# Attention gradients for one query: the products with q and grad_out written as wide matmuls, their scores turned back by transposes

## The chip, the cores and the metric

The kernel runs on one core of one Trainium2 chip. The metric is the device time of one execution in microseconds; before the change the median of three runs is 1302.17 us (1299.8 to 1305.56). The engines of a core named here are TensorE (PE in the profile, with its weight loads as PEld), VectorE (DVE), ScalarE (ACT), GpSimd (POOL) and SyncE (SP). Each works through its own list of instructions in order; semaphores tie the lists together.

## The reference, cut to what matters

Attention with a single query per head, 2 x 32 heads, 8192 keys, head size 128, all in bfloat16, together with the gradients for q, k and v:

```python
B, H, Sq, Sk, D = 2, 32, 1, 8192, 128

def _fwd_reference(q, k, v):
    scale = q.shape[-1] ** -0.5
    scores = jnp.einsum("bhqd,bhkd->bhqk", q, k) * scale
    p = _softmax(scores, axis=-1)
    return jnp.einsum("bhqk,bhkd->bhqd", p, v)

def reference(q, k, v, grad_out):
    _out, _vjp = jax.vjp(_f, q, k, v)      # _f calls _fwd_reference
    _grads = _vjp(grad_out)
    return (_out, *_grads)                 # out, dq, dk, dv
```

For each head this is: scores s = K q, weights P = softmax(s * scale), out = P V, dP = V grad_out, dS = P (dP - sum(P dP)) * scale, dq = dS K, and the two large outputs dv = P grad_out (an outer product) and dk = dS q (another). K and V are 134 MB each and are read once; dk and dv are as large and are written once.

## The kernel before

The 64 heads are handled as 32 pairs. K (or V) of a pair is one tile of 128 partitions x 128 tokens x 128 numbers in the `ring`, 4096 KB; partitions 0 to 63 hold the first head of the pair, 64 to 127 the second. There are six ring tiles, so three pairs fit. The gradients take the place of the inputs: dV is written over V's tile and dK over K's; `outer` (L272) overwrites the chunks that the pair no longer needs, and `store` (L282) sends it out. `load` (L107) of pair g+3 goes into the tile that the store of pair g has emptied; loads are issued by SP, which waits in order for the landing of that store, and stores are issued by ACT between its other work.

The order is written out by hand (`manual_schedule`). An iteration h has 16 steps j, each with two half-steps u. Steps 0 to 7 go through K of pair h in chunks of 16 tokens per partition, steps 8 to 15 through V. Each half-step does, for 8 tokens per partition:

- `transposes` (L113): eight matmuls with the identity (L119) that turn 128 tokens x 128 numbers into 128 x 128 in PSUM, tile `tp` (two buffers);
- the eviction of `tp` to the bfloat16 tile `ev` (four buffers), by ACT (L126), or by DVE (L124) in the first half of steps 8, 9, 10 and 11;
- `products` (L129), one step later: eight times the turned block is loaded as the weights (L136) and two columns, q (or grad_out) of the pair's two heads, stream through. The results land in PSUM tile `sm` (scores) or `dp` directly with tokens on partitions, which is the layout that the later work wants.

While iteration h runs, the second half of pair h-1 is still under way: the counter s is j for the pair of this iteration and j + 16 for the pair before it. The softmax is spread over steps 8 to 11: `row_max` (L154), `all_max` (L159), `exps` (L165), `sums` (L185), `weights_v` (L205), which writes the weights `wz` and the doubled weights `P2` (`doubled`, L197). From s = 12 on, `weighted_rows` (L243) multiplies the weights with the rows of V (and later K) on PE: four matmuls of 512 columns with 16 weight columns each, placed in four column strips of the array, collected in PSUM tile `acc`. `outer` (L272) runs on DVE one step behind. `deltas` (L215) and `weights_k` (L229) do the same for dS when the products with grad_out are finished (steps 0 and 1 of the next iteration). `acc_to_sbuf` (L256) copies `acc` after step 6 of the next iteration, `combine` (L260) at step 8 folds it into the columns of out and dq, and `spread_row` (L140), with a copy by ACT (L152), spreads a row of q or grad_out over the partitions at steps 8 and 2. Which s does what is in these tables:

```python
    ACC_V = {12: (0, 1), 13: (2, 3), 14: (4, 5), 15: (6,), 16: (7,)}
    OUT_V = {12: (0,), 13: (1, 2), 14: (3,), 15: (4, 5), 16: (6,), 17: (7,)}
    ACC_K = {19: (0, 1), 20: (2, 3), 21: (4, 5), 22: (6, 7)}
    OUT_K = {19: (0, 1), 20: (2,), 21: (3, 4), 22: (5,), 23: (6, 7)}
    STORE = {18: 0, 24: 1}
```

The last pair stores its gradients in pieces of 1024 KB as they become ready; at the very end out and dq are turned and stored (L364 to L369).

Of the kernel before, what the change touches and what calls it, by code (L numbers as in the profile page):

```python
# [20 lines left out]
def kernel(  # L21
# [30 lines left out]
    masks.make_identity(nc, ident_f[:])  # L52
    ones_row = const.tile([1, P], F32)
    nc.vector.memset(ones_row[:], 1.0)
    block = const.tile([P, P], F32)
# [31 lines left out]
    acc = ps_one.tile([P, 4 * D], F32, name="acc", tag="acc")  # L87
    sm = ps_one.tile([P, 4 * P], F32, name="sm", tag="sm")
    dp = ps_one.tile([P, 4 * P], F32, name="dp", tag="dp")
    misc = ps_one.tile([P, 4 * P], F32, name="misc", tag="misc")  # L90
# [3 lines left out]
    nat = const.tile([BH, 2, D], BF16)  # L94
    wz = [const.tile([P, NT // 4, 16], BF16, name=f"wz{w}") for w in range(2)]

    class Pair:
# [11 lines left out]

    def scores(w):  # L110
        return (dp if w else sm)[:, 0 : 2 * NT].rearrange("p (s n) -> p s n", s=2)

    def transposes(g, j, u):  # L113
        x = pairs[g]
        w, c = divmod(j, NCH)
        tp = ps_tp.tile([P, HC, P], F32, name="tp", tag="tp")
        for i in range(HC):
            n = c * CH + u * HC + i
            nc.tensor.matmul(  # L119
                tp[:, i, :], lhsT=x.kv[w][:, n, :], rhs=ident_bf[:], start=True, stop=True  # L120
            )
        ev = evp.tile([P, HC, P], BF16, name="ev", tag="ev")
        if (j, u) in ((8, 0), (9, 0), (10, 0), (11, 0)):
            nc.vector.tensor_copy(out=ev[:], in_=tp[:])  # L124
        else:
            nc.scalar.copy(out=ev[:], in_=tp[:])  # L126
        x.ev[j, u] = ev

    def products(g, j, u):  # L129
        x = pairs[g]  # L130
        w, c = divmod(j, NCH)
        ev = x.ev.pop((j, u))
        cols = (qT_all, doT_all)[w][:, 2 * g : 2 * g + 2]
        for i in range(HC):
            n = c * CH + u * HC + i
            nc.tensor.matmul(  # L136
                scores(w)[:, :, n], lhsT=ev[:, i, :], rhs=cols, start=True, stop=True
            )

    def spread_row(g, w):  # L140
# [13 lines left out]
    def row_max(x):  # L154
        x.mp = work.tile([P, 1], F32, name="mp", tag="mp")
        for s, hs in enumerate(halves):
            nc.vector.reduce_max(out=x.mp[hs], in_=scores(0)[hs, s, :], axis=AX.X)  # L157

    def all_max(x):  # L159
        mT = sm[0:1, 2 * NT : 2 * NT + P]  # L160
        nc.tensor.transpose(mT, x.mp[:], ident_f[:])
# [3 lines left out]
    def exps(x):  # L165
        mb = sm[:, 2 * NT + P : 2 * NT + P + 2]
        nc.tensor.matmul(mb, lhsT=ones_row[:], rhs=x.gm[:], start=True, stop=True)  # L167
        negm = work.tile([P, 1], F32, name="negm", tag="negm")
        x.E = big.tile([P, NT], F32, name="E_f", tag="E_f")
        x.ld = work.tile([P, 2], F32, name="ld", tag="ld")  # L170
        for s, hs in enumerate(halves):
            nc.vector.tensor_scalar(
                out=negm[hs], in0=mb[hs, s : s + 1], scalar1=-scale, scalar2=None, op0=ALU.mult
            )
        for s, hs in enumerate(halves):
            nc.scalar.activation(  # L176
                out=x.E[hs],
                in_=scores(0)[hs, s, :],
                func=ACT.Exp,
                bias=negm[hs],  # L180
                scale=scale,
                accum_out=x.ld[hs, 0:1],
            )

    def sums(x, w):  # L185
        x.lsum = (dp if w else sm)[:, 2 * NT + P + 8 : 2 * NT + P + 9]
        nc.tensor.matmul(x.lsum, lhsT=block[:], rhs=x.ld[:, w : w + 1], start=True, stop=True)  # L187

    def to_weights(x, w, src, s1):
        for s, hs in enumerate(halves):  # L190
            nc.vector.tensor_scalar(  # L191
                out=wz[w][hs, :, 8 * w + 4 * s : 8 * w + 4 * s + 4],
                in0=src[hs].rearrange("p (m j) -> p m j", j=4),
                scalar1=s1[hs], scalar2=None, op0=ALU.mult,
            )

    def doubled(x, name, src, s1):  # L197
        t = big.tile([P, NT, 2], BF16, name=name, tag=name)
        nc.vector.tensor_scalar(
            out=t[:], in0=src[:].unsqueeze(2).to_broadcast([P, NT, 2]),  # L200
            scalar1=s1[:], scalar2=None, op0=ALU.mult,
        )
        return t
# [11 lines left out]
    def deltas(x):  # L215
        x.dSu = big.tile([P, NT], F32, name="dSu", tag="dSu")
        for s, hs in enumerate(halves):
            nc.vector.tensor_tensor_reduce(  # L218
                out=x.dSu[hs],
                in0=x.E[hs],  # L220
                in1=scores(1)[hs, s, :],
                scale=1.0,
# [6 lines left out]
    def weights_k(x):  # L229
# [5 lines left out]
        for s, hs in enumerate(halves):  # L235
            nc.vector.scalar_tensor_tensor(  # L236
                out=x.dSu[hs], in0=scores(1)[hs, s, :], scalar=negdelta[hs], in1=x.E[hs],
                op0=ALU.add, op1=ALU.mult,
# [55 lines left out]
    for t in wz:  # L294
        nc.gpsimd.memset(t[:], 0.0)
    nc.vector.memset(acc[:], 0.0)
    for src, dst in ((nat[:, 0, :], qT_all), (nat[:, 1, :], doT_all)):
        tps = ps_tp.tile([P, BH], BF16, name="tps", tag="tp")
# [3 lines left out]

    ACC_V = {12: (0, 1), 13: (2, 3), 14: (4, 5), 15: (6,), 16: (7,)}
    OUT_V = {12: (0,), 13: (1, 2), 14: (3,), 15: (4, 5), 16: (6,), 17: (7,)}
    ACC_K = {19: (0, 1), 20: (2, 3), 21: (4, 5), 22: (6, 7)}
    OUT_K = {19: (0, 1), 20: (2,), 21: (3, 4), 22: (5,), 23: (6, 7)}
    STORE = {18: 0, 24: 1}

    with tc.manual_schedule():
        for g in range(RING // 2):  # L310
            load(g, 0)
            load(g, 1)
        for h in range(NP + 1):
            y = pairs[h] if h < NP else None
            x = pairs[h - 1] if h else None
            for j in range(NS):
                at = [(z, zg, s) for z, zg, s in ((x, h - 1, j + NS), (y, h, j)) if z]
                for u in range(2):
# [6 lines left out]
                    if u == 0:  # L325
                        if y and j == 8:
                            spread_row(h, 0)
                        if x and j == 2:
                            spread_row(h - 1, 1)
                        if x and j == 8:  # L330
                            combine(h - 1)
                    else:
                        if y and j == 9:
                            all_max(y)
                        if y and j == 10:
                            exps(y)
                        if y and j == 11:
                            sums(y, 0)
                        if x and j == 1:
                            sums(x, 1)  # L340
                    if u == 1:
                        for z, zg, s in at:
                            for w, when in ((0, ACC_V), (1, ACC_K)):
                                for c in when.get(s, ()):
                                    weighted_rows(z, w, c)
                if y and j == 8:
                    row_max(y)
                if y and j == 11:
                    weights_v(y)
                if x and j == 0:  # L350
                    deltas(x)
                if x and j == 1:
                    weights_k(x)
                for z, zg, s in at:
# [4 lines left out]
                    for w, when in ((0, OUT_V), (1, OUT_K)):  # L359
                        for c in when.get(s, ()):  # L360
                            outer_and_store(zg, w, c)
                if x and j == 6:
                    acc_to_sbuf(x)
# [36 lines left out]
```

## Time and profile before

| what | before |
|---|---|
| median of three runs | 1302.17 us (1299.8 to 1305.56) |
| profiled execution: time, span | 1301.66 us, 1299.9 us |
| PE busy, weight loads | 1093.5 us, 936.6 us |
| DVE, ACT, POOL busy | 930.0 us, 906.3 us, 2.0 us |
| mean granted clock of TensorE | 0.850 |
| bytes moved by DMA | 539.64 MB, mean 415 GB/s |
| transposes L119 | 8192 matmuls, 721.9 us busy |
| products L136 | 8192 matmuls, 364.6 us busy; their weight loads 338.3 us |
| evictions | ACT 896 x 1020 ns, DVE 128 x 1225 ns |
| outer products on DVE L275 | 512 x about 1220 ns |
| copy of `acc` on DVE L258 | 32 x 692 ns |

The page has six parts: busy time by engine, the span in 40 slices, the DMA queues, the chain of work that ended last, the costliest groups of instructions with the idle time before them, and the DMA issues. From the trace come the same things for any stretch of time, and the instructions in order of time. A row of the order of time gives start, duration, engine, source line, operation, tiles and shapes, and in brackets the idle time ahead of it with what ended it. Matmul durations overlap, so the pace is read from start to start. The granted clock is 1.00 at full speed.

### The profile page before, as it was taken

The numbers are of one execution on the slowest core, as the hardware profiler recorded it, in microseconds if no ns is written. First come the engines' busy times: TensorE is split into PE (matmuls) and PEld (weight loads), VectorE is DVE, ScalarE is ACT, GpSimd is POOL, SyncE is SP. The second block draws the span as 40 slices with busy tenths as digits, with TensorE's granted clock in tenths as the row PEclk, the third lists the DMA queues.
The fourth block names the chain that finished last, engine by engine and source line by source line (L and its number), as shares of the span: only waits on it lengthen the run. The fifth ranks groups of instructions, "written<-read, shape, count | busy, mean of one in ns | idle before, by whom it ended". The sixth has DMA issues, their size and how long they took to land.

```text
span 1299.9 us, 42160 instructions
## 1 busy us (share of the span) xinstructions
PE 1093.5 (84%) x19044; PEld 936.6 (72%) x19044; DVE 930.0 (72%) x1355; ACT 906.3 (70%) x1091; POOL 2.0 (0%) x10
## 2 busy tenths in 40 slices
PE   4999899988888889888888887898888988889883
PEld 3777787776777778777677776677677877778771
DVE  0888788767867677767786676776677666776775
ACT  4887778767866678757686576876578666786761
POOL 0000000000000000000000000000000000000000
PEclk9999989889988788868898688988788777887876
DMA  9999999999999999999999999999999999999986
GB/s 404 417 425 424 429 427 432 427 430 430 429 429 427 427 426 420 427 430 403 426 429 427 429 400 429 432 423 423 414 393 420 416 405 410 410 421 419 404 348 268
DMA packets 19796, 539.64 MB, mean 415 GB/s; under 512 B 2464, under 2 KB 2464, under 8 KB 2464
## 3 DMA queue, kind: packets, MB, share of 16 engines
q10 hardware_dynamic: 10400, 268.51, 49.0%
q1 hardware_dynamic: 9216, 268.44, 48.8%
q8 instruction: 149, 2.44, 0.7%
q14 instruction: 31, 0.25, 0.0%
HBM read 268.47 MB, written 268.47 MB: 413 GB/s over the span
## 4 chain that ended last, share of the span: by engine, by line
DMA 63%; PE 24%; ACT 7%; DVE 3%; issue 2%; ACTq 0%; SPq 0%; DVEq 0%
DMA ring<-in_v_dram 43%; DMA out_dram<-ring 19%; PE tp L119 15%; ACT ev L126 5%; PE misc L264 3%; PE dp L136 2%; PE acc L247 1%; DVE ring L275 1%; DMA nat<-in_grad_out_dram 1%; PE sm L136 1%; DVE ev L124 1%; PE sm L167 1%; ACT E_f L176 1%; ACT row L152 1%; PE sm L187 0%
## 5 line engine op out<-in xcount | busy, mean ns | idle before, releaser
L126 ACT CAST ev<-tp 128x1024 bf16<-128x1024 f32 x896 | 865.4, 1020 | 287.0 <-PE tp L119 273.4
L119 PE MATMUL tp<-ident_bf,ring 128*128 128x128 bf16 x8192 | 721.9, 240 | 148.7 <-DMA ring<-in_v_dram 73.8
L119 PEld LDWEIGHTS <-ring 128*128 128x128 bf16 x8192 | 581.3, 108 | 286.7 <-issue 189.6
L136 PEld LDWEIGHTS <-ev 128*128 128x128 bf16 x8192 | 338.3, 100 | 7.3 <-issue 5.7
L275 DVE TENSOR_TENSOR ring<-row,dS 128x2048 bf16<-128x2048 bf16 x256 | 298.9, 1220 | 41.7 <-PE acc L247 39.9
L275 DVE TENSOR_TENSOR ring<-row,P 128x2048 bf16<-128x2048 bf16 x256 | 300.2, 1221 | 36.8 <-PE acc L247 35.8
L124 DVE CAST ev<-tp 128x1024 bf16<-128x1024 f32 x128 | 156.7, 1225 | 135.1 <-PE tp L119 131.6
L136 PE MATMUL dp<-doT_all,ev 128*128 128x2 bf16 x4096 | 185.7, 167 | 2.2 <-issue 1.4
L136 PE MATMUL sm<-qT_all,ev 128*128 128x2 bf16 x4096 | 178.9, 165 | 3.8 <-issue 3.7
L247 PE MATMUL acc<-ring,wz 128*16 128x512 bf16 x2048 | 167.8, 396 | 3.2 <-DVE wz L191 2.3
L152 ACT CAST row<-misc 128x128 bf16<-128x128 f32 x64 | 18.1, 282 | 81.5 <-PE misc L143 74.8
L264 PE MATMUL misc<-pick,accsb 128*128 128x4 f32 x256 | 52.0, 326 | 17.5 <-ACT row L152 11.2
L264 PEld LDWEIGHTS misc<-pick,accsb 128*128 128x128 f32 x256 | 49.2, 286 | 23.2 <-ACT row L152 16.0
L247 PEld LDWEIGHTS <-wz 128*16 128x16 bf16 x2048 | 31.2, 86 | 11.0 <-issue 2.7
L218 DVE CUSTOM_DVE_ANT_0 dSu<-E_f,dp 64x128 f32<-64x128 f32 x64 | 18.3, 285 | 28.5 <-PE dp L136 28.0
L157 DVE TENSOR_REDUCE mp<-sm 64x1 f32<-64x128 f32 x64 | 18.5, 289 | 21.9 <-PE sm L136 21.2
L268 DVE CAST colsT<-misc 128x4 bf16<-128x4 f32 x32 | 5.1, 161 | 31.8 <-PE misc L264 31.8
L176 ACT ACTIVATE E_f<-sm,negm 64x128 f32<-64x128 f32 x64 | 23.2, 363 | 1.7
L236 DVE SCALAR_TENSOR_TENSOR dSu<-dp,negdelta,E_f 64x128 f32<-64x128 f32 x64 | 22.4, 350 | 2.2
L258 DVE COPY accsb<-acc 128x512 f32<-128x512 f32 x32 | 22.1, 692 | 2.0 <-PE acc L247 1.0
L191 DVE TENSOR_SCALAR wz<-dSu,rl 64x128 bf16<-64x128 f32 x64 | 18.1, 283 | 2.1
L191 DVE TENSOR_SCALAR wz<-E_f,rl 64x128 bf16<-64x128 f32 x64 | 18.1, 283 | 1.7
(42 smaller groups left out, 197.6 us busy)
## 6 DMA issues: line engine op xcount, KB each, us to landing
out_dram<-ring ACTq DMA_DIRECT2D x62, 4096.0 KB, 45.9
ring<-in_k_dram SPq DMA_DIRECT2D x32, 4096.0 KB, 27.6
ring<-in_v_dram SPq DMA_DIRECT2D x32, 4096.0 KB, 27.8
out_dram<-ring ACTq DMA_DIRECT2D x8, 1024.0 KB, 11.3
out_dram<-rows ACTq DMA_DIRECT2D x2, 16.0 KB, 9.7
nat<-in_q_dram ACTq DMA_DIRECT2D x1, 16.0 KB, 11.0
nat<-in_grad_out_dram ACTq DMA_DIRECT2D x1, 16.0 KB, 15.4
```

What stands on the lines that cost most here:

```text
L119: nc.tensor.matmul(tp[:, i, :], lhsT=x.kv[w][:, n, :], rhs=ident_bf[:], start=True, stop=True)
L124: nc.vector.tensor_copy(out=ev[:], in_=tp[:])
L126: nc.scalar.copy(out=ev[:], in_=tp[:])
L136: nc.tensor.matmul(scores(w)[:, :, n], lhsT=ev[:, i, :], rhs=cols, start=True, stop=True)
L152: nc.scalar.copy(out=x.row[:], in_=pb)
L176: nc.scalar.activation(out=x.E[hs], in_=scores(0)[hs, s, :], func=ACT.Exp, bias=negm[hs], scale=scale, accum_out=x.ld[hs, 0:1],)
L191: nc.vector.tensor_scalar(out=wz[w][hs, :, 8 * w + 4 * s : 8 * w + 4 * s + 4], in0=src[hs].rearrange("p (m j) -> p m j", j=4), scalar1=s1[ ...
L236: nc.vector.scalar_tensor_tensor(out=x.dSu[hs], in0=scores(1)[hs, s, :], scalar=negdelta[hs], in1=x.E[hs], op0=ALU.add, op1=ALU.mult,)
L247: nc.tensor.matmul(acc[32 * g : 32 * g + 16, :], lhsT=wz[w][:, n // 4, :], rhs=rows[:, n : n + 4, :].rearrange("p n d -> p (n d)"), start= ...
L258: nc.vector.tensor_copy(out=x.accsb[:], in_=acc[:])
L264: nc.tensor.matmul(c, lhsT=x.accsb[:, j * D : (j + 1) * D], rhs=pick[:, j], start=(j == 0), stop=(j == 3),)
L275: nc.vector.tensor_tensor(out=x.kv[1 - w][:, n : n + CH, :].rearrange("p n (d t) -> p n d t", t=2), in0=row.unsqueeze(1).to_broadcast([P, ...
```

## The change

`products` no longer loads the turned block as weights. The two columns of q (or grad_out) become the weights, and the turned blocks stream: four blocks of 128 tokens, 512 columns, in one matmul. So that all chunks can share one PSUM tile, the two columns stand in a block of 16 that is otherwise zero; which two of the 16 depends on the chunk c, so that chunk c adds its scores into rows 2c and 2c+1 and zero into the others. The zero-padded weights are `qz` (one for q, one for grad_out, 8 x 18 columns), refilled for each pair by `stand` on GpSimd. A half-step issues two such matmuls, in column strips 2u and 2u+1 of the array, and the whole of K (or V) collects in one tile `raw`, started at c = 0 and stopped at c = 7.

The scores then lie with tokens along the free axis. `raw_to_sbuf` copies `raw` to SBUF on DVE (fp32, into a buffer of the `ev` pool), and `turn_scores` transposes it by four fp32 transposes into PSUM tile `turned`, one tile for both inputs. The order of the tokens in it is another, so everything that reads scores or writes weights has new access patterns, and `doubled` becomes two instructions. `row_max`, `all_max`, `exps`, `sums`, `weights_v`, `deltas`, `weights_k`, the tables and the stores move one step later; `acc_to_sbuf` moves from step 6 to 8 and `combine` from 8 to 9. VectorE evicts (3,0), (10,0), (11,0), (12,0) instead of (8,0), (9,0), (10,0), (11,0). The small PSUM results of the softmax move into `misc`. On DVE the order around step 8 is now: outers up to dK chunk 5, copy of `raw`, outers 6 and 7, copy of `acc`.

```diff
-    sm = ps_one.tile([P, 4 * P], F32, name="sm", tag="sm")
-    dp = ps_one.tile([P, 4 * P], F32, name="dp", tag="dp")
+    raw = ps_one.tile([P, 4 * P], F32, name="raw", tag="raw")
+    turned = ps_one.tile([P, 4 * P], F32, name="turned", tag="turned")
...
+    qz = [const.tile([P, 8 * 18], BF16, name=f"qz{w}") for w in range(2)]
...
-    def scores(w):
-        return (dp if w else sm)[:, 0 : 2 * NT].rearrange("p (s n) -> p s n", s=2)
+    def scores(s):
+        hs = halves[s]
+        return turned[hs].rearrange("p (k r z) -> p z k r", k=16, z=2)[:, s, :, 0:8]
+
+    def by_rounds(t):
+        return t.rearrange("p (k r) -> p k r", r=8)
+
+    def by_tokens(t):
+        return t.rearrange("p (i g r) -> p r g i", i=4, g=4)
...
-        if (j, u) in ((8, 0), (9, 0), (10, 0), (11, 0)):
+        if (j, u) in ((3, 0), (10, 0), (11, 0), (12, 0)):
             nc.vector.tensor_copy(out=ev[:], in_=tp[:])
...
+    def stand(g, w):
+        cols = (qT_all, doT_all)[w][:, 2 * g : 2 * g + 2]
+        nc.gpsimd.tensor_copy(
+            out=qz[w][:].rearrange("p (r c) -> p r c", c=18)[:, :, 0:2],
+            in_=cols.unsqueeze(1).to_broadcast([P, 8, 2]),
+        )
...
-        for i in range(HC):
-            n = c * CH + u * HC + i
-            nc.tensor.matmul(
-                scores(w)[:, :, n], lhsT=ev[:, i, :], rhs=cols, start=True, stop=True
-            )
+        for i in range(2):
+            k = 2 * u + i
+            nc.tensor.matmul(
+                raw[32 * k : 32 * k + 16, :],
+                lhsT=qz[w][:, 16 * c : 16 * c + 16],
+                rhs=ev[:, 4 * i : 4 * i + 4, :].rearrange("p n d -> p (n d)"),
+                start=(c == 0),
+                stop=(c == NCH - 1),
+                tile_position=(0, 32 * k),
+            )
+
+    def raw_to_sbuf(x):
+        x.raw = evp.tile([P, 4 * P], F32, name="rawsb", tag="ev")
+        nc.vector.tensor_copy(out=x.raw[:], in_=raw[:])
+
+    def turn_scores(x):
+        for i in range(4):
+            own = slice(i * P, (i + 1) * P)
+            nc.tensor.transpose(turned[:, own], x.raw[:, own], ident_f[:])
...
     def doubled(x, name, src, s1):
         t = big.tile([P, NT, 2], BF16, name=name, tag=name)
-        nc.vector.tensor_scalar(
-            out=t[:], in0=src[:].unsqueeze(2).to_broadcast([P, NT, 2]),
-            scalar1=s1[:], scalar2=None, op0=ALU.mult,
-        )
+        for k in range(2):
+            nc.vector.tensor_scalar(
+                out=t[:, :, k].rearrange("p (r g i) -> p r g i", g=4, i=4),
+                in0=by_tokens(src[:]), scalar1=s1[:], scalar2=None, op0=ALU.mult,
+            )
         return t
...
-    ACC_V = {12: (0, 1), 13: (2, 3), 14: (4, 5), 15: (6,), 16: (7,)}
-    OUT_V = {12: (0,), 13: (1, 2), 14: (3,), 15: (4, 5), 16: (6,), 17: (7,)}
-    ACC_K = {19: (0, 1), 20: (2, 3), 21: (4, 5), 22: (6, 7)}
-    OUT_K = {19: (0, 1), 20: (2,), 21: (3, 4), 22: (5,), 23: (6, 7)}
-    STORE = {18: 0, 24: 1}
+    ACC_V = {13: (0, 1), 14: (2, 3), 15: (4, 5), 16: (6,), 17: (7,)}
+    OUT_V = {13: (0,), 14: (1, 2), 15: (3,), 16: (4, 5), 17: (6,), 18: (7,)}
+    ACC_K = {20: (0, 1), 21: (2, 3), 22: (4, 5), 23: (6, 7)}
+    OUT_K = {20: (0, 1), 21: (2,), 22: (3, 4), 23: (5,), 24: (6, 7)}
+    STORE = {19: 0, 25: 1}
+    stand(0, 0)
...
-                        if x and j == 2:
+                        if x and j == 3:
                             spread_row(h - 1, 1)
-                        if x and j == 8:
+                        if x and j == 9:
                             combine(h - 1)
                     else:
                         if y and j == 9:
+                            turn_scores(y)
+                        if y and j == 10:
                             all_max(y)
-                        if y and j == 10:
+                        if y and j == 11:
                             exps(y)
-                        if y and j == 11:
+                        if y and j == 12:
                             sums(y, 0)
                         if x and j == 1:
+                            turn_scores(x)
+                        if x and j == 2:
                             sums(x, 1)
...
+                if y and j == 4:
+                    stand(h, 1)
+                if h + 1 < NP and j == 12:
+                    stand(h + 1, 0)
                 if y and j == 8:
+                    raw_to_sbuf(y)
+                if x and j == 0:
+                    raw_to_sbuf(x)
+                if y and j == 9:
                     row_max(y)
-                if y and j == 11:
+                if y and j == 12:
                     weights_v(y)
-                if x and j == 0:
+                if x and j == 1:
                     deltas(x)
-                if x and j == 1:
+                if x and j == 2:
                     weights_k(x)
...
-                if x and j == 6:
+                if x and j == 8:
                     acc_to_sbuf(x)
```

## The prediction

> **What bounds the kernel now.** I read the page's part 1 and 2 first, then the DMA queues, then the chain, then the busy time by stretches, and last the order of time inside two early pairs. The page:
>
> ```profile
> span 1299.9 us, 42160 instructions
> DMA  9999999999999999999999999999999999999986
> q10 hardware_dynamic: 10400, 268.51, 49.0%
> q1 hardware_dynamic: 9216, 268.44, 48.8%
> q8 instruction: 149, 2.44, 0.7%
> DMA 63%; PE 24%; ACT 7%; DVE 3%; issue 2%; ACTq 0%; SPq 0%; DVEq 0%
> ```
>
> Loads and stores together fill the 16 DMA engines for 97.8% of the span, so a pair (four transfers of 4096 KB, 16.78 MB) costs 39.0 us at the 430 GB/s of the best slices and 40.4 us at the mean of 415. The engines' shares (PE 84%, ACT 70%) look far away. The stretches show how far:
>
> ```profile
> 80.00:120.00 40.00, 36.63 (x702) 30.88 (x699) 33.47 (x51) 33.34 (x41) 0.00 (x0) 0.96 1.00 417
> 1000.00:1040.00 40.00, 34.72 (x574) 29.86 (x571) 27.91 (x42) 27.27 (x34) 0.00 (x0) 0.79 1.00 410
> ```
>
> (columns: PE, weight loads, VectorE, ScalarE, GpSimd busy; then granted clock, DMA share, GB/s). Early, with three pairs loaded ahead, 702 matmuls fit in 40 us at clock 0.96; later 574 at 0.79. Two successive `combine` groups (L264) start at 65.70 and 100.13: compute alone needs 34.4 us per pair. Between the first V transposes of pair 1 (64.38) and of pair 31 (1251.39) lie 30 pairs of 39.6 us. So DMA sets the pace, and compute has 39.6 - 34.4 = 5.2 us to spare per pair. The question is whether the change uses up more than that. The order of time in an early pair:
>
> ```profile
> 111.12 6.90 DVE L275 TENSOR_TENSOR ring<-row,P 128x2048 bf16<-128x2048 bf16 x6 [0.55 <-PE acc L247]
> 111.88 0.61 PE L119 MATMUL tp<-ident_bf,ring 128*128 128x128 bf16 x8
> 112.32 0.34 PE L136 MATMUL dp<-doT_all,ev 128*128 128x2 bf16 x8
> 112.60 0.61 PE L247 MATMUL acc<-ring,wz 128*16 128x512 bf16 x8
> 113.14 0.62 PE L119 MATMUL tp<-ident_bf,ring 128*128 128x128 bf16 x8
> 116.54 0.39 PE L247 MATMUL acc<-ring,wz 128*16 128x512 bf16 x4
> 116.86 0.10 PEld L119 LDWEIGHTS <-ring 128*128 128x128 bf16 x1 [0.23 <-issue]
> ...
> 63.23 0.69 DVE L258 COPY accsb<-acc 128x512 f32<-128x512 f32 x1
> 63.84 2.35 DVE L275 TENSOR_TENSOR ring<-row,dS 128x2048 bf16<-128x2048 bf16 x2
> 64.38 0.61 PE L119 MATMUL tp<-ident_bf,ring 128*128 128x128 bf16 x8 [0.33 <-ACT ev L126]
> 65.70 1.06 PE L264 MATMUL misc<-pick,accsb 128*128 128x4 f32 x8 [0.36 <-ACT row L152]
> 66.61 0.61 PE L119 MATMUL tp<-ident_bf,ring 128*128 128x128 bf16 x8
> 68.38 0.61 PE L119 MATMUL tp<-ident_bf,ring 128*128 128x128 bf16 x8 [0.98 <-ACT ev L126]
> 69.03 1.01 PE L119 MATMUL tp<-ident_bf,ring 128*128 128x128 bf16 x8
> ```
>
> From start to start at full clock: eight transposes 0.44 us, eight products 0.20, a `weighted_rows` group of four 0.27 (0.32 alone; the next weight load waits for it). ScalarE's evictions follow each other every 0.98 us and pace most half-steps. The 1.01 us row is the half clock (0.86 from start to start), which holds from 69.0 to 72.8 after PE had paused only 0.36 and 0.98 us.
>
> **The change part by part.** I write (j,u) for half-step u of step j, T for its eight transposes, P for its products. Sums are per pair against the 34.4 us.
>
> Products. Per half-step 8 weight loads and 8 two-column matmuls go; 2 loads of 16 columns and 2 matmuls of 512 columns in two column strips come. Nearest row: a lone L247 group, 0.32 us; with two strips I take 0.30 against 0.20. Bounds: 0.21 (the streaming alone) to 0.52 (the two one after the other). Under ScalarE's 0.98 pace it is hidden (0.44 + 0.30). It shows in the seven steps with two L247 groups, 2 x 0.74 + 0.54 = 2.02 against ScalarE's 1.96: from T(4,1) to T(8,0) I get 7.2 us against 6.65 (before, a late pair: 1038.95 to 1045.6, where V then makes PE wait): **+0.55**.
>
> V section, first half. The order on VectorE is now: copy of `raw`, the last two dK outers (6 and 7), copy of `acc`; before, `acc` was copied two steps ahead of `combine`. `combine` at (9,0) stands on PE behind T(8,0), P(7,0), T(8,1), P(7,1), T(9,0), P(8,0). From T(8,0): P(7,1) ends at 1.65; semaphore 0.15, `raw` 0.69, outers 2.35, `acc` 0.69, 0.1: `combine` at 5.6, done at 6.4, then T(9,1). Before it was 64.38 to 69.03 = 4.65: **+1.75**. PE and then ScalarE sit idle some 2.7 us. P(8,0) itself waits for the `raw` copy (one PSUM tile serves both inputs), inside this time.
>
> V section, second half. The turn adds four fp32 transposes after P(8,1). Their cost has no row: per transpose, bounded below by an fp32 weight load of 0.10 (L264: eight passes in 0.80) and above by a half-clock load and stream in series, 0.19 + 0.23 = 0.42. I take 0.16 at full clock, nearer the L264 pace since loads can overlap, so 0.65 per turn. Then (10,0), (11,0), (12,0) go to VectorE at 1.23 each with the maximum, exponent and sum steps one step later. Walking the waits, T(12,0) starts 11.6 us after T(8,0) with no slow clock; before 74.75 - 64.38 = 10.4, of which the 3.8 us at half clock cost about 1.7. After an idle stretch of 2.7 us I expect half clock again, over `combine` (+0.7), T(9,1) and its products (+0.6), the turn and one more half-step (+0.7): 2.0 us, so 13.6. First and second half together: **+3.2** (without slow clock +1.2).
>
> K section. VectorE now runs, from the last dO product on: `raw` copy 0.12 + 0.69, two outers 2.35, `deltas` 0.65, an outer 1.2, negdelta and `dSu` 1.0, `wz` 0.6, the two halves of `doubled` 0.6 (a 128-element row is 0.28, before one of 0.35), an outer 1.2, and only then the eviction of (3,0), 8.4 to 9.65. T(3,0) is done about 5.5, and P(3,0) stops PE until 9.7. T(0,0) to T(4,1) becomes 11.7 us against 9.67 (47.73 to 57.40), the second turn included: **+2.1**. PE is half idle for 4 us there, so half clock may follow in the PE-paced steps: 0 to 1.5, I take **+0.75**.
>
> Last quarter, T(12,0) to the next T(0,0): 7.8 against 8.0: **0** (one more eviction on VectorE, products slower).
>
> Sum 34.4 + 0.55 + 3.2 + 2.1 + 0.75 = **41.0 us per pair**. Low end, clock never slow: 38.1. High end: slow clock for 8 us after each V, as in the last pair of before (1252.7 to 1260.6), and products 0.1 dearer where PE paces: 44.
>
> Costed at nothing: `stand`, 64 small GpSimd copies four steps or more ahead of their use (cover: those steps; price without it about 0.2 each, as GpSimd's 128x128 memset). The stores, their issues on ACT's queue and the loads behind them on SP move a step and the stall later, about 4 to 6 us; the cover is the store queue, 45.9 us to landing where 4096 KB alone at 415 GB/s take 10.1. Without it the DMA would run dry for those 4 to 6 us, twice a pair. The products go from 16,384 instructions to 4096, some 900 others come: 27% of 42,160 fewer, which shorten q8's 0.7% (9 us) by 2.5 us, worth something only if DMA still bounds.
>
> Ends. Pair 0 takes 30.8 us (16.9 to 47.7), now about 2.5 more: T(8,0) of pair 1 at 69 instead of 64.4. From T(8,0) of pair 31 to the end were 48.5 us; the V section, a `raw` copy and turn ahead of `deltas` (+2) and `acc` copied after the last outers make it 53.
>
> **Sum.** 69 + 30 x 41.0 + 53 = 1352 us of span. Around the span lie 1.8 us (profiled run 1301.66, span 1299.9), and that run is 0.5 below the median 1302.17: **1354 us**.
>
> **Rivals.** *DMA still covers it.* If compute stays under 39.6 us per pair, last V lands where it did, less 2.5 for instruction traffic, plus 4.5 of tail: 1302 + 2 = 1304. For it: a 100% DMA share and a walk whose margin over 39.6 is only 1.4 us. Against: two stalls that follow from in-order queues. Chance 0.10.
>
> *The clock stays full.* If PE never falls to half clock, the sum is 38.1, again under DMA's 39.6, and the time about 1304. Against it is the fall at 69.0 after pauses of 0.36 and 0.98 us, which the coming stall of 2.7 exceeds. Chance 0.05. The Trainium skill, "TensorE: Matmul & The Clock Gate", section "HAM oscillation — how this bites in real kernels", asks for no PE gaps above about 3.4 us; by that rule the 2.7 us stall would be harmless and this rival right, but the trace disagrees, with half clock after 0.98.
>
> *Faster.* The other side: the products now stream 512 columns, so PE is denser at half clock and returns sooner; V waits (73.8 us in 25 pairs) and the half-clock spells of some 13 us per late pair shrink, stores issue earlier and DMA holds its best rate. It decides once compute stays under 38 us per pair, and gives 64 + 30 x 39.0 + 53 + 2 = 1289. Against: DMA was full at 410 GB/s too. Chance 0.07.
>
> *Worse.* Products one after the other, or long half clock: above 42.6 us per pair, beyond 1400, with 44 us 1444. Chance 0.12.
>
> **How the numbers follow.** Forecast 0.66, between 39.6 and 42.6 us per pair. Range 1300 to 1400: it takes in the hidden cases and leaves out 0.07 below and 0.12 above. No change means within 0.5%, 6.5 us, about what can be measured here: 0.10, the hidden cases' larger part. Slower 0.66 + 0.12 + 0.05 = 0.83, faster 0.07.
>
> **What the profile after would show.** DMA share near 0.95 with V waits almost gone; `combine` starts about 41 us apart; `combine` waiting for the VectorE copy of `acc` some 2.5 us in each pair; PE waiting at the products for the VectorE eviction of (3,0); clock about 0.8 to 0.9 in all stretches. I am wrong if V waits stay at 2 us per pair (DMA still bounds) or if product pairs take 0.45 us or more.

## The result, and the profile after

| | before | after |
|---|---|---|
| median | 1303.87 us (1299.8 to 1307.04, 4 runs) | 1431.26 us (1430.55 to 1433.02, 4 runs) |
| profiled execution: time, span | 1301.66 us, 1299.9 us | 1430.55 us, 1428.8 us |
| granted clock, mean | 0.850 | 0.902 |
| mean GB/s | 415 | 377 |
| time per pair, first to 31st start of `combine` | 39.6 us | 43.7 us |

The ratio is 1.0981, 95% interval 1.0946 to 1.1016. The kernel became slower, as forecast, by 127 us where 52 were forecast; 1431 lies above the range of 1300 to 1400.

The page of after, its first line, the DMA row of the 40 slices, the queues and the stores:

```profile
span 1428.8 us, 30765 instructions
...
DMA  9989999989999999999999998999989999999947
...
q1 hardware_dynamic: 9216, 268.44, 47.5%
q10 hardware_dynamic: 10400, 268.51, 44.6%
q8 instruction: 103, 1.69, 0.4%
...
out_dram<-ring ACTq DMA_DIRECT2D x62, 4096.0 KB, 19.9
```

Loads and stores together have fallen from 97.8% of the span to 92.1%, and a store now lands 19.9 us after its issue instead of 45.9. With two stores in each pair, 45.9 us were more than two stores under way at once, 19.9 us in pairs of 43.7 are about one. DMA follows; compute leads. The same two stretches as before (PE, weight loads, VectorE, ScalarE, GpSimd busy; granted clock, DMA share, GB/s):

```profile
80.00:120.00 40.00, 34.69 (x389) 20.39 (x388) 30.01 (x42) 27.91 (x33) 0.40 (x2) 0.93 0.91 368
1000.00:1040.00 40.00, 34.66 (x380) 20.89 (x378) 28.67 (x41) 27.04 (x34) 0.40 (x2) 0.91 0.93 384
```

Early and late are alike, which they were not before: there is no stock of loaded pairs that runs out. The waits (total, times, longest):

```profile
ACT ev L134 <- PE tp L127: 400.0, 433, 14.9
...
PE misc L296 <- DVE accsb L290: 88.7, 32, 8.9
...
DVE rawsb L161 <- ACT row L180: 57.5, 31, 1.9
PE raw L150 <- DVE ev L132: 47.0, 31, 1.5
```

PE's waits for V and K, 73.8 and 5.2 us before, are gone from the list. In their place stand two waits for VectorE, one of each kind per pair: `combine` for the copy of `acc`, and `products` for the eviction of (3,0). The first one in the order of time:

```profile
594.19 0.62 PE L127 MATMUL tp<-ident_bf,ring 128*128 128x128 bf16 x8
...
595.78 0.39 PE L150 MATMUL raw<-ev,qz 128*16 128x512 bf16 x2
...
596.10 0.62 PE L127 MATMUL tp<-ident_bf,ring 128*128 128x128 bf16 x8
596.27 0.69 DVE L161 COPY rawsb<-raw 128x512 f32<-128x512 f32 x1 [1.89 <-ACT row L180]
...
596.88 2.35 DVE L307 TENSOR_TENSOR ring<-row,dS 128x2048 bf16<-128x2048 bf16 x2
...
597.01 0.39 PE L150 MATMUL raw<-ev,qz 128*16 128x512 bf16 x2 [0.29 <-DVE rawsb L161]
...
599.14 0.68 DVE L290 COPY accsb<-acc 128x512 f32<-128x512 f32 x1
...
599.97 1.84 PE L296 MATMUL misc<-pick,accsb 128*128 128x4 f32 x8 [2.58 <-DVE accsb L290]
...
601.67 1.01 PE L127 MATMUL tp<-ident_bf,ring 128*128 128x128 bf16 x8
...
602.62 0.60 PE L150 MATMUL raw<-ev,qz 128*16 128x512 bf16 x2
...
603.15 1.12 PE L166 MATMUL turned<-ident_f,rawsb 128*128 128x128 f32 x4
```

Read down the VectorE rows: copy of `raw`, two outers, copy of `acc`, and only then `combine`, 2.58 us after PE had nothing else to do. The last four rows are PE at half clock (`combine` 1.84 us instead of 1.06, transposes 1.01 instead of 0.62). The second wait, with the store's issue that the ScalarE queue holds in front of an eviction:

```profile
626.79 0.61 PE L127 MATMUL tp<-ident_bf,ring 128*128 128x128 bf16 x8 [0.84 <-ACT ev L134]
...
627.65 1.23 DVE L132 CAST ev<-tp 128x1024 bf16<-128x1024 f32 x1
...
628.08 1.01 ACT L134 CAST ev<-tp 128x1024 bf16<-128x1024 f32 x1 [1.34 <-DVE ring L307]
...
628.92 0.39 PE L150 MATMUL raw<-ev,qz 128*16 128x512 bf16 x2 [1.52 <-DVE ev L132]
...
629.80 1.26 PE L279 MATMUL acc<-ring,wz 128*16 128x512 bf16 x8
...
630.99 1.03 PE L127 MATMUL tp<-ident_bf,ring 128*128 128x128 bf16 x8
```

Again a stall, and behind it half clock. And a step of after where PE is never short of work, with the weight loads:

```profile
612.91 0.62 PE L127 MATMUL tp<-ident_bf,ring 128*128 128x128 bf16 x8
613.46 0.39 PE L150 MATMUL raw<-ev,qz 128*16 128x512 bf16 x2
613.78 0.62 PE L127 MATMUL tp<-ident_bf,ring 128*128 128x128 bf16 x8
614.33 0.39 PE L150 MATMUL raw<-ev,qz 128*16 128x512 bf16 x2
614.34 0.81 PE L279 MATMUL acc<-ring,wz 128*16 128x512 bf16 x8
615.08 0.62 PE L127 MATMUL tp<-ident_bf,ring 128*128 128x128 bf16 x8
```

From start to start: transposes to products 0.55 us, products to transposes 0.32, products with a group of eight `weighted_rows` 0.75; the whole step 2.17 us.

### The profile page after: what moved, and what is told of

It reads as the page before. It is cut to its first block, busy times and chain, and to the rows that moved or that the text cites. A ratio compares the mean times of both kernels' runs of the same rounds, so it can differ in the third digit from the quotient of the medians.

```text
span 1428.8 us, 30765 instructions
## 1 busy us (share of the span) xinstructions
PE 1228.6 (86%) x13220; PEld 751.7 (53%) x13220; DVE 986.0 (69%) x1451; ACT 925.4 (65%) x1091; POOL 15.1 (1%) x76
## 5 line engine op out<-in xcount | busy, mean ns | idle before, releaser
L127 PE MATMUL tp<-ident_bf,ring 128*128 128x128 bf16 x8192 | 683.3, 231 | 26.6 <-ACT ev L134 26.2
L127 PEld LDWEIGHTS <-ring 128*128 128x128 bf16 x8192 | 523.7, 104 | 280.3 <-issue 273.1
L150 PE MATMUL raw<-ev,qz 128*16 128x512 bf16 x2048 | 414.8, 401 | 59.3 <-DVE ev L132 47.0
L279 PE MATMUL acc<-ring,wz 128*16 128x512 bf16 x2048 | 225.9, 404 | 1.2 <-DVE wz L219 1.2
L150 PEld LDWEIGHTS <-qz 128*16 128x16 bf16 x2048 | 98.8, 86 | 174.3 <-issue 76.7
L161 DVE COPY rawsb<-raw 128x512 f32<-128x512 f32 x64 | 44.3, 692 | 121.4 <-PE raw L150 63.8
L296 PE MATMUL misc<-pick,accsb 128*128 128x4 f32 x256 | 50.8, 322 | 88.7 <-DVE accsb L290 88.7
L279 PEld LDWEIGHTS <-wz 128*16 128x16 bf16 x2048 | 51.1, 88 | 34.8 <-issue 9.4
L166 PE MATMUL turned<-ident_f,rawsb 128*128 128x128 f32 x256 | 55.7, 355 | 0.6 <-DVE rawsb L161 0.6
L166 PEld LDWEIGHTS turned<-ident_f,rawsb 128*128 128x128 f32 x256 | 35.4, 175 | 21.3 <-issue 20.2
L215 PE MATMUL misc<-ld,block 128*128 128x1 f32 x128 | 24.5, 260 | 1.8 <-DVE ld L249 1.8
L204 ACT ACTIVATE E_f<-turned,negm 64x128 f32<-64x128 f32 x64 | 23.2, 362 | 1.6
## 6 DMA issues: line engine op xcount, KB each, us to landing
out_dram<-ring ACTq DMA_DIRECT2D x62, 4096.0 KB, 19.9
```

Of the source, the lines that this page charges most:

```text
L127: nc.tensor.matmul(tp[:, i, :], lhsT=x.kv[w][:, n, :], rhs=ident_bf[:], start=True, stop=True)
L150: nc.tensor.matmul(raw[32 * k : 32 * k + 16, :], lhsT=qz[w][:, 16 * c : 16 * c + 16], rhs=ev[:, 4 * i : 4 * i + 4, :].rearrange("p n d -> ...
L161: nc.vector.tensor_copy(out=x.raw[:], in_=raw[:])
L166: nc.tensor.transpose(turned[:, own], x.raw[:, own], ident_f[:])
L204: nc.scalar.activation(out=by_rounds(x.E[hs]), in_=scores(s), func=ACT.Exp, bias=negm[hs], scale=scale, accum_out=x.ld[hs, 0:1],)
L279: nc.tensor.matmul(acc[32 * g : 32 * g + 16, :], lhsT=wz[w][:, n // 4, :], rhs=rows[:, n : n + 4, :].rearrange("p n d -> p (n d)"), start= ...
```

## The experiments

The theory to test: the loss is two waits that the in-order queues make, and the half clock behind each. The rivals: the wide products are themselves dear; the later stores starve DMA; the moved order alone is the loss. The measure that tells most is the time per pair, from one start of `combine` to the next; where neither transfers nor the clock interfere, it mostly repeats to 0.02 us.

**The copy of `acc` a step earlier.**

```diff
-                if x and j == 8:
+                if x and j == 7:
                     acc_to_sbuf(x)
```

> The changed kernel with one edit: the copy of acc is issued after step 7 instead of after step 8, so that on VectorE it stands ahead of the copy of raw and of outers 6 and 7. Theory (stalls): combine waits 2.6 us per pair for that copy and the half clock behind it costs another 2 to 3 us (combine 1.84 instead of 0.8, then the next transposes, products and the turn); both go, 43.7 us per pair becomes about 39, and the time falls from 1431 to between 1303 (DMA's floor) and 1350. Rival (products): TensorE's 0.87 us per half-step, with a switch to column strips and back, sets the pace and the gap is only moved: not below 1400.

Measured: 1298.41 us (10 runs), ratio to before 0.9987 (0.9968 to 1.0005). One moved line takes away 133 us and puts the time a little below the 1303 to 1350 expected. `combine` waits once, 6.6 us at the start of the run, and not again; the wait for (3,0) stays at 47.0 us. The first five pairs take 37.76 us each, later ones up to 42 us, in which PE waits for K again (18.8 us in 13 waits) or runs at half clock behind the smaller stall; stores land after 37.9 us.

**(3,0) evicted by ScalarE.**

```diff
-        if (j, u) in ((3, 0), (10, 0), (11, 0), (12, 0)):
+        if (j, u) in ((10, 0), (11, 0), (12, 0)):
```

> The changed kernel with one edit: the block of (3,0) is evicted by ScalarE instead of VectorE, so ScalarE has one more eviction (0.98 us) and the products of (3,0) no longer wait behind VectorE's long row of work. Theory (stalls): 1.5 us of wait and about 1.3 us of half clock in steps 4 to 7 go, 3 us per pair, time about 1340 (1320 to 1370). Rival (products): the wait moves to the next eviction, not below 1400.

Measured: 1348.91 us (4 runs), ratio 1.0363 (1.0348 to 1.0379), pairs of 40.23 to 41.59 us; `combine` still waits 88.7 us. So the smaller stall is worth 82 us by itself, with the half clock that follows it.

**Both.**

> Both edits, the early copy of acc and ScalarE evicting (3,0). Theory (stalls): 43.7 less 5 less 3 is under DMA's 39.6 us per pair, so the time meets DMA's floor, 1300 to 1312, the same as the kernel before. Rival (products): TensorE alone keeps it above 1380. Rival (later stores): the stores are still issued one step later than before, and if that is what costs, the time stays above 1400.

Measured: 1293.06 us (4 runs), ratio 0.9940 (0.9922 to 0.9957): with the two waits gone, the changed kernel is 0.6% faster than before, and below the 1300 to 1312 expected. The first seven pairs take 36.4 to 36.6 us each, later ones about 40. PE waits for K and V again (total, times, longest):

```profile
PE tp L127 <- DMA ring<-in_k_dram: 45.4, 22, 3.0
PE tp L127 <- DMA ring<-in_v_dram: 16.2, 13, 1.5
```

DMA sets the pace here. Neither the products nor the stores' steps were touched, which ends the later stores as the cause of the 127 us, and dear products as the whole cause. It does not show that the products are cheap: what they cost lies under the cover of DMA here.

**PE kept at work in the larger stall.** Six repeats of T(9,1), into the tile that the real ones then overwrite with the same values, stand ahead of `combine`. The stall stays; PE isn't idle in it.

```diff
+                            if y:
+                                keep_busy(h, 9, 1, 6)
                             combine(h - 1)
...
```

> The changed kernel with the wait of combine left as it is, but TensorE kept busy in it: the eight transposes of (9,1) are issued six times more, into the same PSUM buffer, ahead of combine (6 x 0.44 = 2.6 us). It separates the stall from the slow clock. Theory (stalls and slow clock): the stall stays, the half clock behind it goes, 2 to 3 us per pair less, 1340 to 1375. If the slow clock is of no account: 1425 to 1440. If the repeated work delays combine: above 1440.

Measured: 1365.29 us (4 runs), ratio 1.0497 (1.0479 to 1.0514), 66 us less than after although PE does 48 matmuls more in each pair. The pairs come in three sizes, near 40.39, 41.65 (to 41.86) and 43.07 us. The clock records of the trace tell them apart: a pair of the first size has no half clock in it, one of the second has a spell of 3.41 us (182.91 to 186.32, for one), one of the third a spell of 6.83 us (346.75 to 353.57).

**Only the products.** The kernel before with the two wide strips, written to `sm` and `dp`.

```diff
-        for i in range(HC):
-            n = c * CH + u * HC + i
+        for i in range(2):
+            k = 2 * u + i
             nc.tensor.matmul(
-                scores(w)[:, :, n], lhsT=ev[:, i, :], rhs=cols, start=True, stop=True
+                (dp if w else sm)[32 * k : 32 * k + 16, :],
+                lhsT=qz[w][:, 16 * c : 16 * c + 16],
+                rhs=ev[:, 4 * i : 4 * i + 4, :].rearrange("p n d -> p (n d)"),
...
```

> The kernel before, with its order of steps, its evictions on VectorE and its copy of acc untouched; only the products are the two strips with 512 streamed columns, written into sm and dp. The scores are then not turned: what the later steps read from sm and dp is not the scores, so the turning (raw copy, four transposes) is left out of the time. Theory (in-order stalls and the half clock behind them): wide products alone add some 0.2 us in each half-step that PE paces and no stall, so compute stays at 35 to 36.5 us per pair, under the transfers' 39.6, and the time is 1290 to 1306, against 1302 before. Rival (the wide products are themselves slow, one after the other or dearer to switch to): at least 42 us per pair and above 1370.

Measured: 1286.83 us (4 runs), ratio 0.9877 (0.9849 to 0.9905), a little below what was expected and the shortest time of all; the copies of `raw` and the turn are left out of it. The first five pairs take 34.8 to 34.9 us where before took 34.4 to 35.7. The granted clock from 40 to 240 us is 1.00, before it was 0.95. So in place, wide products cost next to nothing net: they are longer, but PE keeps its clock. The sections of the first five pairs show both sides. From T(12,0) to T(0,0), T(0,0) to T(4,1) and T(4,1) to T(8,0), where both kernels run at clock 1.00, the means go from 8.05, 9.35 and 7.03 us to 8.47, 9.70 and 7.40, 1.1 us more in all. From T(8,0) to T(12,0), where before runs at a mean clock of 0.70 to 0.84 and this kernel at 1.00, the mean goes from 10.64 to 9.25, 1.4 us less.

**Only the moved order.** The old products with the later tables, the later softmax steps, `acc` copied at step 8, `combine` at step 9, and VectorE's evictions as in after.

```diff
-        if (j, u) in ((8, 0), (9, 0), (10, 0), (11, 0)):
+        if (j, u) in ((3, 0), (10, 0), (11, 0), (12, 0)):
...
-                        if x and j == 8:
+                        if x and j == 9:
                             combine(h - 1)
...
-                if x and j == 6:
+                if x and j == 8:
                     acc_to_sbuf(x)
...
```

> The kernel before with its old products, and with all that the change moves: the later tables for outers and stores, acc copied at step 8 and combine at step 9, the steps on scores one later, VectorE's evictions at (3,0), (10,0), (11,0), (12,0). No raw copy and no turn. It computes the same. Theory: combine now waits for VectorE (outers 2.35, acc copy 0.69) but without the raw copy's 0.69 and its wait ahead, so about 1.0 to 1.8 us instead of 2.58; the wait for (3,0) shrinks in the same way to under 1 us. Compute 36.5 to 39.5 us per pair, still hidden: 1295 to 1320. It needs both the moved order and the added VectorE work to reach 43.7 us. Rival (the moved order is the whole loss): 42 us or more per pair, above 1370.

Measured: 1304.92 us (10 runs), ratio 1.0029 (1.0015 to 1.0044). The waits are there, but short; one row of its order of time:

```profile
146.62 1.03 PE L264 MATMUL misc<-pick,accsb 128*128 128x4 f32 x8 [0.94 <-DVE accsb L258]
```

0.94 us instead of 2.58. The first seven pairs take 35.4 to 37.9 us, mean 36.6, and DMA covers them. The moved order alone is not the loss; it needs what else the change adds, the copies of `raw`, the turns and the longer half-steps.

**Four strips together.** After, with the products of both half-steps behind the second one's transposes.

```diff
-                    if y and j:
-                        products(h, j - 1, u)
-                    elif x and j == 0:
-                        products(h - 1, NS - 1, u)
+                    for v in range(2 * u):
+                        if y and j:
+                            products(h, j - 1, v)
+                        elif x and j == 0:
+                            products(h - 1, NS - 1, v)
```

> The kernel after, with the four strips of a step issued together behind the second half-step's transposes, instead of two behind each: one change from full-width weights to 16-column strips per step instead of two. Theory: the two stalls stay, and each step that PE paces gets 0.2 to 0.35 us shorter (one exposed weight load of 0.11 and part of a 0.32 group saved), some 7 to 16 steps: 1 to 3 us per pair, 1340 to 1400, if the products' later place makes no new wait; the evicted blocks are held half a step longer, which may give part back. Rival (the change of strips costs nothing; only stalls and clock do): 1420 to 1440.

Measured: 1346.94 us (4 runs), ratio 1.0347 (1.0322 to 1.0373), 84 us less than after, with both stalls still in place and `combine`'s longer (106.1 us in 32). Pairs average 41.0 us, at 39.3, 40.8 or 42.8. At full clock in both kernels, the section from T(12,0) to T(0,0), which has no stall, takes 7.67 us instead of 8.46 in after, and T(4,1) to T(8,0) 7.06 instead of 7.81. So part of the loss does come from the products, as the rival of dear products had it, through the changes between the whole array and the strips. Two successive waits for (3,0) in its order of time show what differs:

```profile
595.42 0.61 PE L127 MATMUL tp<-ident_bf,ring 128*128 128x128 bf16 x8 [1.90 <-DVE ev L132]
595.95 0.39 PE L150 MATMUL raw<-ev,qz 128*16 128x512 bf16 x4
...
596.71 1.70 PE L127 MATMUL tp<-ident_bf,ring 128*128 128x128 bf16 x16
...
636.09 0.61 PE L127 MATMUL tp<-ident_bf,ring 128*128 128x128 bf16 x8 [1.90 <-DVE ev L132]
636.62 0.39 PE L150 MATMUL raw<-ev,qz 128*16 128x512 bf16 x4
...
637.38 1.07 PE L127 MATMUL tp<-ident_bf,ring 128*128 128x128 bf16 x16
```

The same wait of 1.90 us, once with half clock behind it (16 transposes in 1.70 us), once without (1.07).

**All three.** The copy of `acc` earlier, (3,0) on ScalarE, four strips together.

> The kernel after with acc copied a step earlier, (3,0) evicted by ScalarE, and the four strips of a step together. Theory: transfers bound it already without the fours (1293.06), so 1288 to 1298, combine starts 39.5 to 40.3 us apart once the loads ahead are used up, below 36.4 us early in the run. Rival (the compute side still sets the time): below 1280.

Measured: 1289.82 us (4 runs), ratio 0.9904 (0.988 to 0.9928). The first four pairs take 34.18 us, less than before's shortest, then DMA leads at about 40. Against the 36.43 us of the first pairs with both stalls removed, all at clock 1.00, putting four strips together is worth 2.25 us per pair. Of the versions that do the whole computation this has the shortest time, 1.0% below before.

**PE kept at work in both stalls, first try.** Three repeats of T(4,1) ahead of P(3,0), beside the six of T(9,1).

```diff
+                    if y and x and j == 4 and u == 0:
+                        keep_busy(h, 4, 1, 3)
                     if y and j:
                         products(h, j - 1, u)
```

> The kernel after with both stalls left in and PE kept at work in them: the six repeats of T(9,1) ahead of combine, and three repeats of T(4,1) ahead of P(3,0). Theory: the half clock has two homes, behind combine and behind the wait for (3,0). With only the first filled, pairs took 40.39 us where no half clock followed (3,0) and 41.65 to 43.07 where it did. Filled in both places every pair should take 40.4 us: 1338 to 1350, granted clock 0.98 or more. What is then left above the 36.43 us of the kernel without either stall, 4.0 us, is the stalls themselves. Rival (the longer pairs come from something other than the clock): 1355 to 1370, pairs of 41.65 and 43.07 still there.

Measured: 1396.97 us (4 runs), ratio 1.0730 (1.0703 to 1.0756), outside both expectations. The repeats didn't fall into the stall; this row of its order of time shows why:

```profile
614.45 1.95 PE L147 MATMUL tp<-ident_bf,ring 128*128 128x128 bf16 x24 [1.51 <-DVE ev L135]
```

Their PSUM tile comes free with the same eviction of (3,0) that PE was waiting for. The stall of 1.51 us stayed empty and 1.4 us of work came behind it: pairs of 41.82 (40.39 + 1.43) and of 43.3 us. It says nothing on the clock.

**PE kept at work in both stalls, second try.** The repeats are of T(4,0), just ahead of the wait and with its tile free.

```diff
-        for i in range(HC):
-            n = c * CH + u * HC + i
+        for i in range(4 * HC if g and (j, u) == (4, 0) else HC):
+            n = c * CH + u * HC + i % HC
...
```

> As the last one, with the second filling where it can run: the transposes T(4,0), which stand just ahead of the wait for (3,0) and whose tile is free, are issued four times over (the tile is rewritten with the same values), 3 x 0.44 = 1.3 us of work inside a wait of 1.51. The six repeats of T(9,1) ahead of combine stay. Theory: no half clock behind either stall, so all pairs take the 40.4 us that the undisturbed pairs of the kernel with one filling took: 1338 to 1352, granted clock 0.98 or more. Rival (pairs of 41.65 and 43.07 have another cause): they stay, 1355 to 1370.

Measured: 1330.80 us (4 runs), ratio 1.0223 (1.0197 to 1.0249); mean clock 0.992. That is below the 1338 to 1352 expected, though the pairs are the 40.4 us that were expected. The sizes of 41.65 and 43.07 us are gone: nearly every pair takes 40.38 to 40.40 us. Rows of its order of time, and one stretch:

```profile
597.40 2.85 PE L147 MATMUL tp<-ident_bf,ring 128*128 128x128 bf16 x48
600.09 1.01 PE L311 MATMUL misc<-pick,accsb 128*128 128x4 f32 x8
...
624.40 1.95 PE L130 MATMUL tp<-ident_bf,ring 128*128 128x128 bf16 x32 [0.84 <-ACT ev L137]
```

```profile
240.00:1200.00 960.00, 924.34 (x11523) 597.46 (x11522) 730.02 (x1073) 686.83 (x811) 9.45 (x47) 1.00 1.00 416
```

VectorE's order, which makes both waits, is as in after; PE fills them with 72 needless matmuls in each pair, and the kernel is 100 us faster than after, with a granted clock of 1.00 in the stretch shown. So half clock cost after 100 us, or a little more.

Put in a row, by the time of a pair where no transfer waited (after: the mean from the first to the 31st start of `combine`):

| kernel | us per pair | step |
|---|---|---|
| before, first pairs | 34.4 to 35.7 | |
| wide products alone | 34.8 | about 0 |
| + `raw` copies, turns, moved steps (both waits removed) | 36.4 | 1.6 |
| + the wait for (3,0) (`acc` early) | 37.8 | 1.3 |
| + `combine`'s wait (PE kept at work) | 40.4 | 2.6 |
| + half clock behind the waits (after) | 43.7 | 3.3 |

DMA covers whatever lies below about 39.6 us. Alone, none of the steps up to 37.8 shows in the time; the last two come to 5.9 us, of which 4.1 lie above the cover, times 30 pairs 123 of the 127 us. The steps add up like this only in this order: below the cover a saving shows nothing, and above it several savings overlap. Grouping the strips alone takes 84 us off after, and so the products' cost, here inside the first rows, is one of the causes too.

## Why the prediction was wrong in size

The direction, the place and the two mechanisms stand as forecast. The sum was 69 + 30 x 41.0 + 53; measured it is 70.2 + 30 x 43.68 + 48.2 = 1428.8. The start was 1 us off and the tail 5 the other way; the pair was 2.7 us too short, 80 us in all. By the sections of the sum, with the predicted times, a pair of after with both spells of half clock, and a pair of the kernel with PE at work in both stalls:

| section | forecast, with half clock | after | forecast, full clock | full clock, measured |
|---|---|---|---|---|
| T(8,0) to T(12,0) | 13.6 | 14.6 | 11.6 | 12.1 |
| T(12,0) to T(0,0) | 7.8 | 8.5 | 7.8 | 8.5 |
| T(0,0) to T(4,1) | 11.7 | 12.0 | 11.7 | 12.0 |
| T(4,1) to T(8,0) | 7.95 | 9.3 | 7.2 | 7.8 |
| sum | 41.05 | 44.4 | 38.3 | 40.4 |

**The step that failed is the products' half-step, "0.44 + 0.30" = 0.74 us.** It is 0.55 + 0.32 = 0.87. The 0.32 was right within its bounds; the 0.44, eight transposes with nothing lost behind them, was carried over from before, where the products' weight loads start ahead of the products (112.27 for 112.32 in its order of time). In after they don't:

```profile
613.46 0.09 PEld L150 LDWEIGHTS <-qz 128*16 128x16 bf16 x2
613.77 0.45 PEld L127 LDWEIGHTS <-ring 128*128 128x128 bf16 x8 [0.23 <-issue]
614.33 0.09 PEld L150 LDWEIGHTS <-qz 128*16 128x16 bf16 x2
```

Each load starts only when its products do (613.46, 614.33 in the rows of PE above), and the next full-width load starts when the strips end. The price is some 0.11 us at each change from the whole array to strips. The Trainium skill, "TensorEngine Tiling (Array Packing)", section "Key Properties", says that a change of the tiling mode (not just of the tile) drains TensorE. The trace agrees in so far as the products begin 0.55 us behind the transposes' start and not 0.44; that a drain is what delays the loads is not shown. It is the rule that the prediction should have weighed against the change.

With 0.87 per half-step and 2.17 per step with two groups, PE and no longer ScalarE (1.96) paces these steps. From T(4,1) to T(8,0) lie seven half-steps and four groups of eight `weighted_rows`, each of which adds 0.75 - 0.32 = 0.43: 7 x 0.87 + 4 x 0.43 = 7.81, as measured. The prediction's own terms give 7 x 0.74 + 4 x 0.54 = 7.34, which it put down as 7.2. The last quarter has eight half-steps and three groups; the same terms make it 8 x 0.13 - 3 x 0.11 = 0.7 longer than forecast, all of what was measured. These two sections hold 1.3 of the 2.1 us at full clock. The other 0.8 lies in the two with the stalls: the copy of `raw` starts 2.08 us behind T(8,0) (596.27 for 594.19) where 1.80 was forecast, two half-steps of 0.87 ahead of it; the rest stays open. Grouping the strips takes the last quarter from 8.46 to 7.67 us, which tests the step itself.

Wide products in the kernel before show no such loss because they lose there too, some 1.1 us in three sections, and gain it back in the fourth by keeping the clock.

Two of the prediction's bases came from other pairs than the 34.4 us that they were added to: 9.67 us for T(0,0) to T(4,1) and 6.65 for T(4,1) to T(8,0), where the pair from 64.38 has 9.37 and 6.98. The two slips cancel in the sum, which is luck.

**Half clock was forecast at 2.75 us per pair and cost 3.3.** The terms behind `combine` were right in kind; behind (3,0), where 0.75 was taken from a range of 0 to 1.5, most pairs pay about 1.5 (9.3 against 7.8). At half clock the longer half-step costs more too: 1.50 us (630.99 to 632.49 in after) against 1.07 before (70.30 to 71.37).

Point by point:

- `combine` waits 2.58 us in each pair, forecast "some 2.5". Shown right, and by the kernel with `acc` early shown to be the one whose removal takes off most, 133 us.
- PE waits at the products for (3,0), 1.52 us; shown right. The section was 12.0 for 11.7.
- The turn: 0.58 us at full clock (621.10 to 621.68), forecast 0.65; 0.9 at half clock.
- V waits gone, DMA share near 0.95 (0.92 from 40 to 240 us, 0.95 from there to 1200): as listed.
- The loads and stores that move a step were rightly costed at nothing. The products as dear as 0.45 or more: no, 0.32.
- The rivals: "DMA still covers it" needed less than 39.6 us per pair; even with PE at work in both stalls it is 40.4. "The clock stays full" would have given 1331, as the last experiment shows, not the 1304 worked out from 38.1. The rule of the Trainium skill that is quoted there ("TensorE: Matmul & The Clock Gate", section "HAM oscillation — how this bites in real kernels": no PE gaps above about 3.4 us) would have left a stall of 2.58 us harmless; this trace disagrees, with half clock from 599.30 to 606.12 around that stall's end. "Worse" is what came, at 43.7 us per pair, with half clock behind both stalls, and not by products one after the other. The high end of the working, 44 us, named just what came, slow clock and "products 0.1 dearer where PE paces", but the range was cut below it at 42.6.

## What to carry to other kernels

When DMA covers compute by a few microseconds per round, a change is judged by the sum of everything it adds to the round, and each wait counts twice: once as idle time and once as the slow clock behind it. Look for what stands behind a late copy in each in-order queue: moving one copy of 0.7 us ahead of two outer products was worth 133 us here. When matmuls in column strips are put between full-width ones, count the changes: four strips behind sixteen transposes take 0.33 us (106.22 to 106.55 in the kernel with all three edits), as two behind eight do.

## What the runs showed of the hardware that was not expected

- Four strips take what two take. In the kernel with all three edits, four products and eight `weighted_rows` fill 112.00 to 112.75, 0.75 us, as two products and eight do in after:

```profile
112.00 0.39 PE L150 MATMUL raw<-ev,qz 128*16 128x512 bf16 x4
112.22 0.60 PE L279 MATMUL acc<-ring,wz 128*16 128x512 bf16 x8
112.75 0.62 PE L127 MATMUL tp<-ident_bf,ring 128*128 128x128 bf16 x8
```

- The same idle time does not always bring the same clock: 1.90 us with and without half clock behind it, in successive pairs. With the larger stall filled, three sizes of pair, 1.26 and 2.7 us apart, come from this; with PE at work in both they become one. In the clock records every change stands on a grid of 3.41 us, in the traces of before, of after, of four strips together and of the larger stall filled (half clock in after from 599.30 to 606.12 and from 630.02 to 633.43, the second 9 steps of 3.41 after the first). That the place of a stall on this grid decides between the two outcomes fits these records, but no run tests it.
- Needless matmuls in a stall can pay: 72 of them per pair gave 100 us.
- With DMA leading in both, the kernel with wide products alone moves 425 GB/s between 240 and 1200 us where before moves 421, and ends 1.2% earlier. It has fewer instruction fetches (1.65 MB for 2.44), and their share of the DMA engines falls only from 0.7% to 0.5%, too little for that; where the rest comes from was not tried and stays open.
